# End of attention in an attention + two-MoE kernel: gates of the known rows in a product of their own, weight splits behind the last exponentials and ids, last pack's scores first

## The chip, the cores and the metric

The kernel runs on one core of a Trainium2 chip. The core has five engines that work side by side, each through its own queue in the order of the program: TensorE (PE in the rows; its weight loads are PEld), VectorE (DVE), ScalarE (ACT), GpSimd (POOL) and SyncE (SP, which here only reads registers and starts transfers). Sixteen DMA engines move data between the main memory and the on-chip memory. TensorE's clock is granted at one of two levels, 1.2 or 2.4 GHz; the rows give it as 0.5 or 1.0. The metric is the device time of one execution in microseconds (us), the median of several.

## The reference

Block-causal attention (2 sequences of 576 tokens, 8 heads of 64), whose output of 1152 rows x 512 goes through two mixture-of-experts (MoE) layers. Each layer gives a row to the expert with the largest logit (8 experts, weights 512x1024 and 1024x512), multiplies by a gate, and in the first layer by a second, sigmoid gate. The second layer has a capacity per expert.

```python
scores = np.where(block_i >= block_j, scale * q @ k.T, -1e9)      # blocks of 64
x = softmax(scores) @ v                                           # -> 1152 x 512
logits = x @ w_gate;  e_idx = argmax(logits, 1)
gate_w = softmax(logits)[arange, e_idx];  eom = sigmoid(x @ w_output_gate)
for e in range(E):                                                # first MoE
    h = relu(x[mask] @ w1[e]);  out[mask] = gate_w * eom[mask, e] * (h @ w2[e])
# second MoE: the same on its own weights, without eom, with a capacity per expert
```

## The kernel before

**Attention.** The nine query blocks of a head are put into three packs (numbers 0, 1, 2). For a pack PE computes scores into the tile `s` (`qk_steps`), DVE takes the negative row maximum `mx`, ACT the exponential `p`, PE transposes `p` into the tile `pst` (`transp`), ACT or DVE copies it out as `tp`, PE multiplies by the values (`pv`), ACT copies the result as `ot`, and PE turns it back with the logits of the first MoE beside it (the matrix `mv`). DVE divides by the row sums, into `x1` (the rows) and `lg` (the logits), and adds `lg` to `lg1`. The last two heads, 6 and 7, are interleaved: stages (6,0), (7,0), (6,1), (7,1), (6,2), (7,2). In a row such as `tp_7_2_0` the numbers are head, pack and group; `p1_2` is block 2 of an odd head, `p0_8` block 8 of an even one.

**Known rows.** When pack 0 of head 7 is done, 384 of the 1152 rows have all their logits. The routine `route_first` picks the expert that most of them have (its number is `e`) and finds, for up to 384 of these known rows, where they lie (`ids`), the gates (`gs`) and several tables (`kx`, `tx`, `bm`, `dl`, `oht`, `pi`) that the routing of the other rows needs later. It does so in small steps on DVE with products on PE between them: the counts (L289), the places (L320, L322: `a_selb` with a triangle of ones), then a selection by the one-hot matrix `a_ohp` (L369, L371). The last one has in one product the row numbers and the three bf16 parts of the gate, `rag`, five columns a row tile, each times three groups. Its result is read as `ids` (L374, L375), as the register `e2` (the expert again, L379) and as `gs` (L382). `begin_first` spreads these steps over the end of attention, one piece for each call of `extra_step`. It starts the load of the first weights (4 chunks of 512 KB into `raw`) as soon as `e` is known, gathers the known rows (`xg`, three gathers on POOL's queue) when `ids` is there, and then starts the load of the second weights, four more chunks.

**Splits.** The products of the MoE take float32 numbers as a high and a low part. `split_hi` (ACT, L169) casts a weight chunk to its high part `wh`; `split_lo` (DVE, L187) subtracts that to get `wl`. Chunk 0 of layer 1 is split inside `begin_first`, chunks 1 to 3 after the stages, each held behind an anchor instruction by `issue_after` (an order on one engine's queue, without a wait).

**Order and the start of the MoE.** Around here the order on each queue is made by a list scheduler from the order in which the program is written, these anchors and the dependencies; from `manual_schedule` on it is as written. The first MoE begins with the transposes of the first gathered tile, `px<-ident,xg` (L706). They wait for the gather, and their place in PSUM comes free with the last `lg` of attention (L1459 for head 7, pack 2). ACT then casts `xh`, and the 12 products of 512 columns `ph<-wh,xh` and so on (L719) of a half of layer 1 follow.

Of the kernel before, what the change touches and what calls it, by code (L numbers as in the profile page):

```python
# [8 lines left out]
F32 = mybir.dt.float32  # L9
# [5 lines left out]
ALU = mybir.AluOpType  # L15
AX = mybir.AxisListType
# [16 lines left out]
def kernel(  # L33
# [15 lines left out]
    nc = tc.nc  # L49
    V = nc.vector  # L50
# [4 lines left out]
    P = 128  # L55
# [127 lines left out]
    def split_lo(c, s=0, src=None):  # L183
        i = c + s * KD
        fill()
        fill()
        V.tensor_tensor(wls[i], raw[:, c, :] if src is None else src, whs[i].bitcast(F32), op=ALU.subtract)  # L187

    def split(c, s=0, src=None):

        w = split_hi(c, s, src)
        split_lo(c, s, src)
        return w
# [10 lines left out]
    def gather_rows(dst, table, ids):  # L204
        return nc.gpsimd.indirect_dma_start(out=dst, out_offset=None, in_=table, in_offset=bass.IndirectOffsetOnAxis(ap=ids.bitcast(U32), axis=0))
# [72 lines left out]
    def route_first(m, r, lg, og, eligible, tok, capacity, pst):  # L278
# [65 lines left out]
        yield 0  # L344
        ohp = sm([NA, P], "ohp", BF16)
        for t in range(NA):
            V.tensor_scalar(ohp[:, t, :], i128, pp[:, t : t + 1], BIG, op0=ALU.subtract, op1=ALU.is_equal)
            yield 0
        part = [sm([NA], f"part{i}", BF16) for i in range(3)]
        for _ in gates(sm, ex, og, oh, NA, part):  # L350
            yield 0
        ra = sm([NA, 5], "ra", BF16)
        for j, val in enumerate([thr[:, 0:NA], tok[:, 0:NA]] + part):
            V.tensor_copy(ra[:, :, j], val)
            yield 0
        rb = sm([2], "rb", BF16)
        V.tensor_copy(rb, pid.to_broadcast([P, 2]))
        if G > 1:
            yield 0
            og = ohg[:, :, 0:G].unsqueeze(2)  # L360
# [4 lines left out]
            V.tensor_scalar(rbg, og.to_broadcast([P, NA, 2, G]), pid[:, 0:1], None, op0=ALU.mult)  # L365
        yield 1
        ps = pst()
        for t in range(NA):
            nc.tensor.matmul(ps[:, 0 : 5 * G], ohp[:, t, :], ra[:, t, :] if G == 1 else rag[:, t].rearrange("p j g -> p (j g)"), start=(t == 0), stop=False)  # L369
# [5 lines left out]
        V.tensor_scalar_add(ids[:, G : 2 * G], ps[:, G : 2 * G], float(N))  # L375
        r["ig"], r["io"] = ids[:, 0:G], ids[:, G : 2 * G]
        if m == 1:

            V.scalar_tensor_tensor(out=er, in0=ps[:, 0:1], scalar=0.0, in1=ef, op0=ALU.mult, op1=ALU.add)  # L379
            r["e2"] = nc.sync.value_load(er[0:1, 0:1], min_val=0, max_val=E - 1)  # L380
        gs = sm([G], "gs")
        V.tensor_reduce(out=gs, in_=ps[:, 2 * G : 5 * G].rearrange("p (j g) -> p g j", j=3), op=ALU.add, axis=AX.X)  # L382
        r["gs"] = gs
        yield 1
        if m == 1:
            iof = sm([G], "iof")
            V.tensor_scalar_add(iof, ps[:, G : 2 * G], float(N))
            r["oht"], r["pi"] = spots(sm, iof, G)

        kx = sm([NT, E], "kx")  # L390
# [850 lines left out]
    with ExitStack() as actx:  # L1241
# [7 lines left out]
        def pst():  # L1249
            return ps_t.tile([P, 512], F32, tag="t", name="pst")  # L1250
# [156 lines left out]
        def transp(h, pk, g):  # L1407
            s = st[h]
            grp = [(b, c) for c, bs in groups[pk][g] for b in bs]
            ps = pst()  # L1410
            n = len(grp) * P
            for j, (b, c) in enumerate(grp):
                last[0] = nc.tensor.transpose(ps[:, j * P : (j + 1) * P], s["p"][b][:, c * P : (c + 1) * P], ident).ins  # L1413
# [51 lines left out]

        def begin_first():

            it = Phases(route_first(1, first1, lg1[:, 0:NA, 0:E], lg1[:, 0:NA, E : 2 * E], None, tok_t, None, pst))
# [11 lines left out]
            g = [gather_rows(xg, x1d[0 : NA * P, :], first1["ig"][:, i : i + 1]).ins for i, xg in enumerate(item0["xg"])][0]  # L1480
# [16 lines left out]
        def extra_step():  # L1497
            if behind:
                calls[0] += 1
                if calls[0] in (3, 4):  # L1500
                    return
            while extra:
                try:
                    if behind:
                        with tc.issue_after(last[0]):
                            next(extra[0])
                    else:
                        next(extra[0])
                    return
                except StopIteration:  # L1510
                    extra.pop(0)
# [41 lines left out]
        for i, (h, pk) in enumerate(stages):  # L1553
# [257 lines left out]
```

## Time and profile before

| | |
|---|---|
| median of 3 runs | 416.88 us (416.2 to 418.99) |
| the profiled execution, its own time | 416.57 us |
| its span in the trace | 414.8 us |
| PE / DVE / ACT / POOL busy, share of the span | 93% / 70% / 61% / 25% |
| mean granted TensorE clock | 0.976 of full speed |

The span is the time from the first to the last recorded instruction; what lies around it is 1.8 us. A timeline row has the start, the time from the first start to the last end of the instructions that it merges, the engine, the line, the operation, output and inputs, the count, and in brackets the idle time before it with what ended it. The busy time of PE includes its pipeline, so rows that follow each other overlap; the distance of two starts is what one costs. Attention ends near 140 us; layer 1 of the first MoE starts at 140.12 us.

### The profile page before, as it was taken

To read this page: it belongs to the slowest core of one execution; us is meant where nothing else is said; L and a number is where in the kernel's file an instruction comes from. 1 tells how busy PE (TensorE), PEld (TensorE's weight loads), DVE (VectorE), ACT (ScalarE), POOL (GpSimd) and SP (SyncE) were. 2 spreads that over 40 slices of the span, in tenths; PEclk is the share of its full clock that TensorE was granted. 3 is DMA by queue.
4 is the path that set the end of the run, shared out by engine and by line. 5 is a ranking of instruction groups with operands and counts; after the bars stand their busy time and mean duration, and the time that the engine had idled before them with its cause. 6 is when DMAs were issued, how large, how long until landed. Compare 5 with 4: busy or idle time off the path is not lost. (4 is left out here: it accounts for less than half of the span.)

```text
span 414.8 us, 7835 instructions
## 1 busy us (share of the span) xinstructions
PE 386.4 (93%) x2443; PEld 295.3 (71%) x2443; DVE 289.4 (70%) x755; ACT 254.1 (61%) x531; POOL 101.6 (25%) x211
## 2 busy tenths in 40 slices
PE   4899999999996899999999999978999999999992
PEld 3677887887775678888888866656777888856540
DVE  4577667766788697798988944679789999911010
ACT  2678778878775552877878611553679998821110
POOL 8452201212100204103212110121710287200100
PEclk9999999999997999999999999978899999999998
DMA  6649932510106802991661388360795999899890
GB/s 139 114 105 285 294 103 61 144 24 7 57 22 223 297 3 84 305 345 54 216 242 52 122 335 321 137 228 2 248 384 188 333 371 401 288 384 390 297 362 29
DMA packets 65111, 82.88 MB, mean 200 GB/s; under 512 B 34368, under 2 KB 38976, under 8 KB 65060
## 3 DMA queue, kind: packets, MB, share of 16 engines
q1 hardware_dynamic: 62180, 72.98, 52.4%
q0 software_dynamic: 2880, 9.31, 6.1%
q8 instruction: 21, 0.34, 0.3%
q14 instruction: 30, 0.25, 0.2%
HBM read 91.57 MB, written 11.80 MB: 249 GB/s over the span
## 5 line engine op out<-in xcount | busy, mean ns | idle before, releaser
L187 DVE TENSOR_TENSOR wl<-raw,wh 128x1024 fp32r<-128x1024 f32 x52 | 61.3, 1220 | 2.3 <-ACT wh L169 2.3
L169 ACT CAST wh<-raw 128x1024 fp32r<-128x1024 f32 x52 | 51.5, 1052 | 1.0 <-DMA raw<-in_moe_w_dram 0.8
L719 PE MATMUL ph<-wh,xh 128*128 128x512 f32 x120 | 50.7, 422 | 1.4 <-ACT xh L708 1.4
L719 PE MATMUL ph<-wh,xl 128*128 128x512 f32 x120 | 48.6, 405 | 0.0
L719 PE MATMUL ph<-wl,xh 128*128 128x512 f32 x120 | 48.2, 402 | 0.0
L1387 DVE TENSOR_REDUCE mx<-s 128x1 f32<-128x256 f32 (+8 forms) x72 | 34.4, 486 | 17.5 <-PE s L1386 4.6
L1390 ACT ACTIVATE p<-s,mx 128x256 f32<-128x256 f32 (+8 forms) x72 | 37.8, 527 | 10.1 <-DVE mx L1387 9.2
L1413 PE MATMUL pst<-ident,p 128*128 128x128 f32 x200 | 39.1, 291 | 0.4 <-DVE lg L1459 0.3
L187 DVE TENSOR_TENSOR wl_a<-raw,wh_a 128x1024 fp32r<-128x1024 f32 x28 | 33.2, 1220 | 0.3 <-ACT wh_a L169 0.2
L1439 PE MATMUL pst<-tp,vn 128*64 128x128 f32 (+2 forms) x384 | 32.8, 297 | 0.1
L169 ACT CAST wh_a<-raw 128x1024 fp32r<-128x1024 f32 x28 | 28.1, 1061 | 5.8 <-DMA raw<-in_moe_w_dram 5.7
L733 PE MATMUL py<-wh_a,hh 128*128 128x512 f32 x72 | 30.1, 418 | 0.0
L1413 PEld LDWEIGHTS pst<-ident,p 128*128 128x128 f32 x200 | 25.4, 150 | 6.1 <-issue 2.4
L1417 ACT COPY tp<-pst 128x384 f32<-128x384 f32 (+1 forms) x48 | 24.5, 533 | 8.2 <-PE pst L1413 7.9
L733 PE MATMUL py<-wh_a,hl 128*128 128x512 f32 x72 | 28.7, 399 | 0.6 <-DVE hl L814 0.6
L733 PE MATMUL py<-wl_a,hh 128*128 128x512 f32 x72 | 28.8, 401 | 0.0
L187 DVE TENSOR_TENSOR wl_b<-raw,wh_b 128x1024 fp32r<-128x1024 f32 x24 | 28.4, 1220 | 0.6 <-ACT wh_b L169 0.5
L1386 PE MATMUL s<-kh,qh 128*128 128x320 f32 (+3 forms) x64 | 26.0, 406 | 2.7 <-ACT p L1390 1.4
L719 PEld LDWEIGHTS ph<-wh,xh 128*128 128x128 f32 x120 | 23.2, 193 | 6.4 <-ACT xh L708 1.9
L738 POOL DMA_INDIRECT out_dram<-ys,ig x7 | 11.9, 1705 | 63.5 <-ACT ys L921 57.1
L719 PEld LDWEIGHTS ph<-wh,xl 128*128 128x128 f32 x120 | 23.1, 192 | 6.1 <-DVE xl L709 1.3
L1439 PEld LDWEIGHTS pst<-tp,vn 128*64 128x64 f32 x384 | 21.1, 142 | 8.7 <-issue 3.8
(353 smaller groups left out, 868.9 us busy)
## 6 DMA issues: line engine op xcount, KB each, us to landing
raw<-in_moe_w_dram SPq DMA_DIRECT2D x132, 512.0 KB
rx<-in_moe_w_dram SPq DMA_DIRECT2D x20, 512.0 KB
out_dram<-zrow SPq DMA_DIRECT2D x9, 256.0 KB
x2d<-zrow SPq DMA_DIRECT2D x9, 256.0 KB
kn<-in_k_dram SPq DMA_DIRECT2D x16, 128.0 KB
qn<-in_q_dram SPq DMA_DIRECT2D x16, 128.0 KB
vn<-in_v_dram SPq DMA_DIRECT2D x16, 128.0 KB
x1d<-x SPq DMA_DIRECT2D x3, 576.0 KB
```

The source lines that it names most:

```text
L169: nc.scalar.copy(whs[i], raw[:, c, :] if src is None else src)
L187: V.tensor_tensor(wls[i], raw[:, c, :] if src is None else src, whs[i].bitcast(F32), op=ALU.subtract)
L719: yield nc.tensor.matmul(out_, l[:, c * P : (c + 1) * P], r[:, cols], start=(c == 0 and j == 0), stop=(c == KD - 1 and j == 2))
L733: nc.tensor.matmul(y, l[:, cs], r[:, rs], start=(first and j == 0), stop=(last and j == 2))
L738: nc.gpsimd.indirect_dma_start(out=dest, out_offset=bass.IndirectOffsetOnAxis(ap=io.bitcast(U32), axis=0), in_=ys, in_offset=None, bounds_ ...
L1386: nc.tensor.matmul(ps[:, a:z], s[l][:, b, :], s[r][:, a - o : z - o], start=(j == 0), stop=(j == 2))
L1387: anchors["mx", h, pk] = V.tensor_reduce(out=s["mx"][:, t : t + 1], in_=ps[:, o : o + n], op=ALU.max, axis=AX.X, negate=True).ins
L1390: anchors["p", h, pk] = nc.scalar.activation(s["p"][b][:, 0:n], ps[:, o : o + n], AF.Exp, bias=s["mx"][:, t : t + 1], accum_out=s["sm"][:, ...
L1413: last[0] = nc.tensor.transpose(ps[:, j * P : (j + 1) * P], s["p"][b][:, c * P : (c + 1) * P], ident).ins
L1417: anchors["tp", h, pk] = nc.scalar.copy(fp, ps[:, 0:n]).ins
L1439: nc.tensor.matmul(po[r, 0 : n * BLK], nat["v"][h % NR["v"]][:, c, r], w[:, :, r], start=(c == 0), stop=(c == nc_ - 1))
```

## The change

In `route_first`, for the first MoE, the selection becomes two products. The first has only the two row-number columns (`rag[:, :, 0:2]`, six columns of output) beside the `rbg` product, and `ids`, `e2` and `iof` come from it. The gates, their three parts and the second product (`rag[:, :, 2:5]`, nine columns) come after that, then `gs`; `oht`, `pi` and the tables stand behind. `begin_first` issues the two later pieces behind `first1["found"]`, the step that writes `iof` (on DVE), and leaves the rest of the generator (`first1["more"]`: `oht`, `pi`, `kx`, `tx`, `ne`, `bm`, `dl`, `efs`) for the end. `extra_step` also skips its sixth call. In the stage before the last, all scores of the last pack are issued first; in the last stage one piece of `begin_first` is issued at once, behind the transposes of (6,2). All four `split_hi` now follow the stages: chunks 0 and 1 behind the last exponential `p` of (7,2), chunk 2 behind the last ACT copy `tp`, chunk 3 behind the last `ot`. The `split_lo` of chunk 0 is held behind `found`, those of 1 and 2 behind `weighed` (the second `rag`), and the rest of the generator behind the `split_lo` of chunk 2.

```diff
@@ route_first
-        for _ in gates(sm, ex, og, oh, NA, part):
-            yield 0
         ra = sm([NA, 5], "ra", BF16)
-        for j, val in enumerate([thr[:, 0:NA], tok[:, 0:NA]] + part):
+        for j, val in enumerate([thr[:, 0:NA], tok[:, 0:NA]] + (part if G == 1 else [])):
...
-            V.tensor_tensor(rag, ra.unsqueeze(3).to_broadcast([P, NA, 5, G]), og.to_broadcast([P, NA, 5, G]), op=ALU.mult)
+            V.tensor_tensor(rag[:, :, 0:2], ra[:, :, 0:2].unsqueeze(3).to_broadcast([P, NA, 2, G]), gg.to_broadcast([P, NA, 2, G]), op=ALU.mult)
...
+        if G > 1:
+            for _ in gates(sm, ex, og, oh, NA, part):
+                yield 0
+            for j, val in enumerate(part):
+                V.tensor_copy(ra[:, :, 2 + j], val)
+                yield 0
+            r["weighed"] = V.tensor_tensor(rag[:, :, 2:5], ...).ins
+            yield 1
+            ps = pst()
+            for t in range(NA):
+                nc.tensor.matmul(ps[:, 0 : 3 * G], ohp[:, t, :], rag[:, t, 2:5].rearrange("p j g -> p (j g)"), start=(t == 0), stop=(t == NA - 1))
+            yield 0
+            V.tensor_reduce(out=gs, in_=ps[:, 0 : 3 * G].rearrange("p (j g) -> p g j", j=3), op=ALU.add, axis=AX.X)
+            yield 1
@@ begin_first, extra_step
-            it.one()
-            for _ in it.small():
-                pass
-            yield
-            with tc.issue_after(g):
-                item0["w1"] = [split(0)]
+            for _ in range(2):
+                with tc.issue_after(first1["found"]):
+                    it.one()
+                    for _ in it.small():
+                        pass
+                yield
...
-                if calls[0] in (3, 4):
+                if calls[0] in (3, 4, 6):
@@ the loop over the stages, and what follows it
+            if i + 2 == len(stages):
+                for _ in qs_:
+                    pass
+            if i + 1 == len(stages):
+                last[0] = anchors["turn", H - 2, 2]
+                extra_step()
...
-        for c, (w, h, pk) in ((1, ("ot", H - 1, 1)), (2, ("tp", H - 1, 2)), (3, ("ot", H - 1, 2))):
-            with tc.issue_after(anchors[w, h, pk]):
-                item0["w1"].append(split(c) if c < KD - 1 else split_hi(c))
+        item0["w1"] = []
+        for c, w in enumerate(("p", "p", "tp", "ot")):
+            with tc.issue_after(anchors[w, H - 1, 2]):
+                item0["w1"].append(split_hi(c))
+            if c < KD - 1:
+                with tc.issue_after(first1["weighed" if c else "found"]):
+                    at = split_lo(c)
+        with tc.issue_after(at):
+            for _ in Phases(first1["more"]).small():
+                pass
```

The queues before and after, at three places. First ACT's queue at the end of attention, of the kernel before from the copy of (6,2)'s transposes on: `p1_2` is the last exponential of all, `wh0` to `wh2` are the high parts of the weight chunks, `tp_7_2_0` and `tp_7_2_1` the copies that the last product with the values needs.

```order
L1417 COPY tp_6_2_1_1977<-pst_1972 128x512
L169 CAST wh0_108<-raw_107 128x1024
L169 CAST wh1_109<-raw_107 128x1024
L1390 ACTIVATE p1_2_171,sm7_1598<-s_7_2_1890,mx7_1597 128x192
L1417 COPY tp_7_2_0_2035<-pst_2031 128x384
L1417 COPY tp_7_2_1_2045<-pst_2040 128x512
L169 CAST wh2_110<-raw_107 128x1024
```

The same place of ACT's queue with the change, from the copies `ot0` of (6,2) on:

```order
L1461 COPY ot0_189<-pst_2016 64x64
L1407 ACTIVATE p1_2_171,sm7_1598<-s_7_2_1890,mx7_1597 128x192
L169 CAST wh0_108<-raw_107 128x1024
L169 CAST wh1_109<-raw_107 128x1024
L1434 COPY tp_7_2_0_2014<-pst_2010 128x384
L1434 COPY tp_7_2_1_2024<-pst_2019 128x512
L169 CAST wh2_110<-raw_107 128x1024
```

The two casts `wh0` and `wh1` stood ahead of the last exponential and stand behind it now, ahead of the two copies. Next DVE's queue, of the kernel before, from the remainder `wl2` of the third chunk to the last sum of the logits `lg1`; `x1` and `lg` with `pst_2037` belong to (6,2), with `pst_2073` to (7,2).

```order
L187 TENSOR_TENSOR wl2_114<-raw_107,wh2_110 128x1024
L1457 TENSOR_TENSOR x1_145<-pst_2037,ri6_1402 128x3x64
L1459 TENSOR_TENSOR lg_6_2_2070<-pst_2037,ri6_1402 128x48
L1457 TENSOR_TENSOR x1_145<-pst_2073,ri7_1599 128x3x64
L1459 TENSOR_TENSOR lg_7_2_2130<-pst_2073,ri7_1599 128x48
L1461 TENSOR_TENSOR lg1_105<-lg1_105,lg_7_2_2130 128x48
```

With the change the remainders `wl0`, `wl1`, the step `a_gs` and `wl2` come first, then sixteen small steps of `route_first`, of which the last eight are shown, and then the last `x1` and `lg` of (7,2):

```order
L453 COPY a_efs_1_2142<-a_ef_1_1841 128x3
L272 TENSOR_TENSOR a_oht_1_2121<-a_gt_1_2119 128x27
L274 TENSOR_REDUCE a_pi_1_2123<-a_gt_1_2119 128x3
L411 SCALAR_TENSOR_TENSOR a_kx_1_2126<-a_kp_1_1911,a_kx_1_2126 128x24
L418 TENSOR_SCALAR a_tx_1_2129<-a_tx_1_2129 128x72
L436 TENSOR_TENSOR bms_100<-bms_100,a_ne_1_2132 128x64
L447 TENSOR_TENSOR a_dl_1_2136<-a_dl_1_2136,a_ne_1_2132 128x8
L275 SCALAR_TENSOR_TENSOR a_pi_1_2123<-a_pi_1_2123,a_iof_1_2007 128x3
L1474 TENSOR_TENSOR x1_145<-pst_2052,ri7_1599 128x3x64
L1476 TENSOR_TENSOR lg_7_2_2108<-pst_2052,ri7_1599 128x48
```

So all sixteen, which before stood several microseconds earlier and between other work, are now between `wl2` and the last `x1`. Last PE's queue of the kernel before, where (6,2) is transposed (`pst_1899`) and the places of the known rows are computed (L320):

```order
L1413 MATMUL pst_1868<-ident_68,p1_6_175 128x128
L1413 MATMUL pst_1899<-ident_68,p0_8_168 128x128
L1413 MATMUL pst_1899<-ident_68,p0_3_163 128x128
L1439 MATMUL pst_1905<-tp_7_1_0_1810,vn1_152 64x192 x2
L1413 MATMUL pst_1899<-ident_68,p0_2_162 128x128
L1439 MATMUL pst_1905<-tp_7_1_1_1859,vn1_152 64x128 x4
L1439 MATMUL pst_1905<-tp_7_1_2_1871,vn1_152 64x128 x2
L1386 MATMUL s_7_2_1890<-kh7_1595,qh1_155 128x256
L1386 MATMUL s_7_2_1890<-kl7_1596,qh1_155 128x256
L1386 MATMUL s_7_2_1890<-kh7_1595,ql1_157 128x256
L320 LDWEIGHTS ltri_74
L320 MATMUL pst_1913<-a_selb_1_1847,ltri_74 128x4
```

And with the change:

```order
L1430 MATMUL pst_1868<-ident_68,p1_6_175 128x128
L320 LDWEIGHTS ltri_74
L320 MATMUL pst_1904<-a_selb_1_1847,ltri_74 128x4
L322 LDWEIGHTS ones_bf_73
L322 MATMUL pst_1904<-a_selb_1_1847,ones_bf_73 128x3
```

The places of the known rows moved ahead of the transposes of (6,2), the product with the values of (7,1) and the scores of 256 columns.

## Rows read from the trace of the kernel before

**Rows 1.** Page, part 2: TensorE's granted clock in 40 equal slices.
```profile
PEclk9999999999997999999999999978899999999998
```
**Rows 2.** Busy us (count) of each engine by stretch, PEclk, DMA share, GB/s.
```profile
126.71:128.87 2.16, 0.58 (x4) 0.41 (x3) 2.16 (x18) 1.92 (x5) 0.00 (x0) 1.00 0.85 332
128.87:135.70 6.83, 5.56 (x41) 4.37 (x43) 5.13 (x20) 2.85 (x6) 1.49 (x2) 0.50 0.40 146
135.70:140.12 4.42, 2.92 (x32) 2.27 (x28) 2.40 (x7) 2.96 (x9) 2.36 (x3) 1.00 0.94 329
...
275.64:282.47 6.83, 6.83 (x28) 5.07 (x28) 5.14 (x25) 2.84 (x4) 0.12 (x1) 0.50 0.23 89
289.30:292.71 3.41, 3.41 (x10) 2.64 (x9) 3.41 (x4) 3.19 (x4) 3.10 (x2) 0.50 0.31 82
```
**Rows 3.** Timeline of PE at the end of attention and the start of the MoE.
```profile
122.42 0.60 PE L1413 MATMUL pst<-ident,p 128*128 128x128 f32 x4
122.95 0.55 PE L1439 MATMUL pst<-tp,vn 128*64 128x192 f32 x4
...
123.69 0.88 PE L1439 MATMUL pst<-tp,vn 128*64 128x128 f32 x12
125.06 0.39 PE L1386 MATMUL s<-kh,qh 128*128 128x256 f32 x1 [0.49 <-ACT p L1390]
...
125.51 0.18 PE L320 MATMUL pst<-a_selb,ltri 128*128 128x4 bf16 x1
...
127.16 0.27 PE L1386 MATMUL s<-kh,ql 128*128 128x192 f32 x1
130.14 0.19 PE L369 MATMUL pst<-a_rag,a_ohp 128*128 128x15 bf16 x1 [2.71 <-DVE a_ohp L347]
...
138.78 0.63 PE L706 MATMUL px<-ident,xg 128*128 128x128 f32 x4 [0.68 <-DVE lg L1459]
140.12 0.50 PE L719 MATMUL ph<-wh,xh 128*128 128x512 f32 x1 [0.72 <-ACT xh L708]
```
**Rows 4.** Timeline of DVE in the same stretch.
```profile
122.78 0.75 DVE L1387 TENSOR_REDUCE mx<-s 128x1 f32<-128x576 f32 x1
...
124.96 0.18 DVE L317 TENSOR_REDUCE a_selb<-a_oe 128x3 bf16<-128x24 f32 x1
...
127.70 0.28 DVE L399 SCALAR_TENSOR_TENSOR a_tx<-a_eo,a_kq,thr 128x72 f32<-128x72 f32 x1
...
128.67 1.22 DVE L187 TENSOR_TENSOR wl<-raw,wh 128x1024 fp32r<-128x1024 f32 x1
...
133.45 0.16 DVE L374 CAST a_ids<-pst 128x3 int32<-128x3 f32 x1 [0.99 <-PE pst L371]
...
138.20 0.36 DVE L1457 TENSOR_TENSOR x<-pst,ri 128x192 f32<-128x192 f32 x1 [0.35 <-PE pst L1454]
```
**Rows 5.** Timeline of ACT in the same stretch.
```profile
129.50 0.41 ACT L1390 ACTIVATE p<-s,mx 128x192 f32<-128x192 f32 x1
...
134.46 0.59 ACT L1417 COPY tp<-pst 128x512 f32<-128x512 f32 x1 [2.45 <-PE pst L1413]
134.94 1.05 ACT L169 CAST wh<-raw 128x1024 fp32r<-128x1024 f32 x1
```
**Rows 6.** Timeline of PE elsewhere: a product with values, layer 1 at either clock.
```profile
103.93 1.22 PE L1439 MATMUL pst<-tp,vn 128*64 128x192 f32 x20
...
141.42 0.39 PE L719 MATMUL ph<-wl,xh 128*128 128x512 f32 x1
141.65 0.40 PE L719 MATMUL ph<-wh,xl 128*128 128x512 f32 x1
...
278.05 0.63 PE L719 MATMUL ph<-wh,xh 128*128 128x512 f32 x1
278.48 0.63 PE L719 MATMUL ph<-wl,xh 128*128 128x512 f32 x1
```
**Rows 7.** The tile `a_ids`, us from the issue of a gather to its landing.
```profile
DMA to landing us min/median/max: 4.6/6.7/7.1
```

More of the change, by code (lines that the diff above doesn't have):

```diff
@@ L186, in split_lo @@
         fill()
-        V.tensor_tensor(wls[i], raw[:, c, :] if src is None else src, whs[i].bitcast(F32), op=ALU.subtract)
+        return V.tensor_tensor(wls[i], raw[:, c, :] if src is None else src, whs[i].bitcast(F32), op=ALU.subtract).ins
     def split(c, s=0, src=None):
@@ L359, in route_first @@
             yield 0
-            og = ohg[:, :, 0:G].unsqueeze(2)
+            gg = ohg[:, :, 0:G].unsqueeze(2)
             rag = sm([NA, 5, G], "rag", BF16)
-            V.tensor_tensor(rag, ra.unsqueeze(3).to_broadcast([P, NA, 5, G]), og.to_broadcast([P, NA, 5, G]), op=ALU.mult)
+            V.tensor_tensor(rag[:, :, 0:2], ra[:, :, 0:2].unsqueeze(3).to_broadcast([P, NA, 2, G]), gg.to_broadcast([P, NA, 2, G]), op=ALU.mult)
             yield 0
             rbg = sm([NA, 2, G], "rbg", BF16)
-            V.tensor_scalar(rbg, og.to_broadcast([P, NA, 2, G]), pid[:, 0:1], None, op0=ALU.mult)
+            V.tensor_scalar(rbg, gg.to_broadcast([P, NA, 2, G]), pid[:, 0:1], None, op0=ALU.mult)
         yield 1
         ps = pst()
+        n = 5 if G == 1 else 2 * G
         for t in range(NA):
-            nc.tensor.matmul(ps[:, 0 : 5 * G], ohp[:, t, :], ra[:, t, :] if G == 1 else rag[:, t].rearrange("p j g -> p (j g)"), start=(t == 0), stop=False)
+            nc.tensor.matmul(ps[:, 0:n], ohp[:, t, :], ra[:, t, :] if G == 1 else rag[:, t, 0:2].rearrange("p j g -> p (j g)"), start=(t == 0), stop=False)
         for t in range(NA):
@@ L374, in route_first @@
         V.tensor_copy(ids[:, 0:G], ps[:, 0:G])
-        V.tensor_scalar_add(ids[:, G : 2 * G], ps[:, G : 2 * G], float(N))
+        r["found"] = V.tensor_scalar_add(ids[:, G : 2 * G], ps[:, G : 2 * G], float(N)).ins
         r["ig"], r["io"] = ids[:, 0:G], ids[:, G : 2 * G]
@@ L380, in route_first @@
             r["e2"] = nc.sync.value_load(er[0:1, 0:1], min_val=0, max_val=E - 1)
+            iof = sm([G], "iof")
+            r["found"] = V.tensor_scalar_add(iof, ps[:, G : 2 * G], float(N)).ins
         gs = sm([G], "gs")
-        V.tensor_reduce(out=gs, in_=ps[:, 2 * G : 5 * G].rearrange("p (j g) -> p g j", j=3), op=ALU.add, axis=AX.X)
         r["gs"] = gs
+        if G == 1:
+            V.tensor_reduce(out=gs, in_=ps[:, 2 * G : 5 * G].rearrange("p (j g) -> p g j", j=3), op=ALU.add, axis=AX.X)
         yield 1
+        if G > 1:
+            for _ in gates(sm, ex, og, oh, NA, part):
+                yield 0
+            for j, val in enumerate(part):
+                V.tensor_copy(ra[:, :, 2 + j], val)
+                yield 0
+            r["weighed"] = V.tensor_tensor(rag[:, :, 2:5], ra[:, :, 2:5].unsqueeze(3).to_broadcast([P, NA, 3, G]), gg.to_broadcast([P, NA, 3, G]), op=ALU.mult).ins
+            yield 1
+            ps = pst()
+            for t in range(NA):
+                nc.tensor.matmul(ps[:, 0 : 3 * G], ohp[:, t, :], rag[:, t, 2:5].rearrange("p j g -> p (j g)"), start=(t == 0), stop=(t == NA - 1))
+            yield 0
+            V.tensor_reduce(out=gs, in_=ps[:, 0 : 3 * G].rearrange("p (j g) -> p g j", j=3), op=ALU.add, axis=AX.X)
+            yield 1
         if m == 1:
-            iof = sm([G], "iof")
-            V.tensor_scalar_add(iof, ps[:, G : 2 * G], float(N))
             r["oht"], r["pi"] = spots(sm, iof, G)
@@ L1412, in transp @@
             for j, (b, c) in enumerate(grp):
-                last[0] = nc.tensor.transpose(ps[:, j * P : (j + 1) * P], s["p"][b][:, c * P : (c + 1) * P], ident).ins
+                last[0] = anchors["turn", h, pk] = nc.tensor.transpose(ps[:, j * P : (j + 1) * P], s["p"][b][:, c * P : (c + 1) * P], ident).ins
             tp = ap4.tile([P, 4, P], F32, tag="tp", name=f"tp_{h}_{pk}_{g}")
@@ L1466, in begin_first @@
         def begin_first():
-            it = Phases(route_first(1, first1, lg1[:, 0:NA, 0:E], lg1[:, 0:NA, E : 2 * E], None, tok_t, None, pst))
+            first1["more"] = route_first(1, first1, lg1[:, 0:NA, 0:E], lg1[:, 0:NA, E : 2 * E], None, tok_t, None, pst)
+            it = Phases(first1["more"])
             for i in range(4):
@@ L1479, in begin_first @@
             item0["xg"] = [XG.next() for _ in range(KN[1])]
-            g = [gather_rows(xg, x1d[0 : NA * P, :], first1["ig"][:, i : i + 1]).ins for i, xg in enumerate(item0["xg"])][0]
+            for i, xg in enumerate(item0["xg"]):
+                gather_rows(xg, x1d[0 : NA * P, :], first1["ig"][:, i : i + 1])
             load_w(w11, w12, first1["e2"], KD, 8)
             yield
-            it.one()
-            for _ in it.small():
-                pass
-            yield
-            with tc.issue_after(g):
-                item0["w1"] = [split(0)]
+            for _ in range(2):
[4 more added lines that the diff above has]
+                yield
         extra = []
```

3 lines of the change are left out of this document (2 added, 1 removed).

## The prediction

> **What bounds the kernel now.** I began with the clock's row of the page [rows 1]. It dips in the slices from 124 to 134 us, from 270 to 300 us and in the last; the first dip lies where the change works. By stretch [rows 2], the clock is full until 128.87, half from there to 135.70, and full again after. PE is busy for only 0.58 of the 2.16 us before the fall. The timeline of PE says why [rows 3]: its last score product starts at 127.16 and ends near 127.43, and the next product (L369, the selection of the known rows) starts at 130.14, after 2.71 us in which PE waited for `a_ohp` from DVE. DVE was late because a weight remainder `wl` of 1.22 us stood ahead of it [rows 4]. So the clock fell 1.44 us after PE had gone idle, and the 5.56 us of busy PE that follow up to 135.70 ran at half.
>
> The second thing to see is where the MoE begins. The transposes `px` start at 138.78, after 0.68 us in which PE waited for the last `lg` on DVE, and `ph`, the first product of layer 1, starts 1.34 us later, at 140.12 [rows 3]. From there on I count every microsecond of PE in full, since its rows follow each other without a pause (starts 0.23 us apart [rows 6]). So two numbers decide: when `ph` starts, and at which clock.
>
> **The change, part by part.** *The early part.* The row numbers now need neither gates nor parts. On DVE the maximum at 122.78 takes 0.75 us [rows 4] and ends at 123.5; in the new queue only one small step, one copy and two reciprocals stand between it and `a_selb`. That step cannot start before 123.5 and before the change started at 124.96 [rows 4]; I take 124.3, nearer the late end because the copy is no small step. PE now has L320 right behind two of the four transposes that start at 122.42 [rows 3], so it is idle from about 122.9 to 124.5: **a new pause of 1.6 us** (0.8 to 2.3 by the same two bounds). Before, other products lay there.
>
> From 124.5 on, PE has until the end of the id products: ten transposes at 0.13 us (four start at 122.42, the next work at 122.95), the products with values of (7,1) at 0.5 and 0.9 us (rows of 122.95 and 123.69), scores of 0.45 us (125.06 to 125.51), and some ten tiny products, 0.4 us by estimate [rows 3]. Sum 3.6 us: 128.1. `ids` then comes at about 128.4 in place of 133.45 [rows 4]: 5 us sooner. This buys little. The gathers take 4.6 to 7.1 us from issue to landing [rows 7], and the first was in time for 138.78 before; now it lands by 136 and nobody waits for it. The second weights come 5 us sooner too, and no row of PE shows a wait for them in layer 1.
>
> *The last exponential.* Behind the ids PE waits for `ot` and turns (7,1) back, 0.8 us (0.4 to 1.2, taken in the middle), multiplies (6,2) by the values, 1.2 us [rows 6], and does the last scores, 0.45 us: 130.5. With the maximum on DVE (0.5 us) the last `p` starts at 131.1. Before it started at 129.50 [rows 5]: though its block is issued first, it is 1.6 us later, because the pause and the id products now lie ahead of it.
>
> *From there to `ph`.* ACT now has `wh0` and `wh1` between the last exponential and the two copies `tp` of (7,2), and `wh2` behind these. DVE has `wl2` and sixteen small steps ahead of the last `x1` and `lg`. In order: `p` 0.5 us, two casts at 1.05, two copies (0.59 and about 0.45), the cast `wh2` 1.05 [rows 5], its remainder `wl2` 1.22, sixteen small steps, and 0.58 from the last `x1` (138.20) to `px` (138.78) [rows 3, 4]. For the sixteen I use the 18 DVE instructions of the 2.16 us from 126.71, 0.12 us each, 1.9 us [rows 2]; the longest of them took 0.28 alone [rows 4]. Sum: 0.5 + 2.1 + 1.05 + 1.05 + 1.2 + 1.9 + 0.6 = 8.4 us, so `px` at 139.5 against 138.78 and `ph` at 140.8 against 140.12: **+0.7 us**. The other branch (`ot` behind `wh2`, the turn back, `x1`) would be ready for `x1` near 137, so it is DVE that is late next. Casts and small steps were covered before, by PE's pause and by its slow stretch; that cover is gone.
>
> *The clock.* Between 132 and 140.8 PE now has pauses of about 2 us (for the copies behind `wh0`, `wh1`), 0.8 us (for `ot`), 2.5 us (for the last `lg`) and 0.8 us (for `xh`), and less than 3 us of work. Before, from 135.70 to 140.12, it was busy for 2.92 of 4.42 us and the clock stayed full; a fall came with 0.58 busy of 2.16 [rows 2]. The new stretch is nearer the second. So layer 1 most likely starts at half clock. Its products start 0.43 us apart there, 0.23 at full [rows 6], so each microsecond at half loses 0.47. Dense work ran 3.41 and 6.83 us at half before the clock came back [rows 2]: 1.6 or 3.2 us lost. I take the middle, **+2.4 us**; the bounds are nothing and 3.2.
>
> The sum is made against the profiled execution's own time, 416.57 us (span 414.8 and 1.8 around it), 0.3 below the median 416.88: 416.57 + 0.7 + 2.4 = 419.7 us.
>
> **Rule and row.** The trace shows a fall 1.44 us after PE went idle, inside a pause of 2.71 us [rows 2, 3]. The Trainium skill (TensorE: Matmul & The Clock Gate, section "HAM oscillation — how this bites in real kernels") gives as its abstract rule that only pauses longer than any of these cost the clock. By it there would be no fall before, which the rows contradict, and none with the change, which gives the time of the first rival.
>
> **The rivals.** *The clock holds.* If pauses with short work between them do not let it fall, only the shift stays: 416.57 + 0.7 = 417.3 us. For it speaks that 135.70 to 140.12, with pauses of 0.7 us, kept the full clock; against it that PE will be busy for much less there. *Slower: the new pause at 122.9 also lets the clock fall.* Its place is L320 behind `a_selb`; it decides if the clock falls in that pause as it did in the one at 128.87. Then the 3.6 us of work up to `ids` runs at 1.9 times its length, wholly or in part: 0 to 3.1 us, middle 1.6, and all behind it is late: 421.3 us. For it speaks the estimate of 1.6 us; against it that PE worked densely right before and after. *Faster: the clock holds and DVE's small steps are cheap.* If they and `wl2` slip in before the last turn back is done, `px` comes when that branch allows, near 137.6, 1.1 us sooner than before: 415.4 us. For it speaks that the stall of 2.71 us is gone; against it the fixed order, in which `wl2` cannot start before the third cast. That the change does nothing is no case here, since `ids` must come sooner; only its use is in doubt.
>
> **How the numbers follow.** Chances: layer 1 at half clock alone 0.42 (419.7), with the early fall too 0.28 (421.3), the clock holds 0.17 (417.3), faster 0.13 (415.4). The likeliest gives the prediction, 419.7. The range goes from the faster case, 415.4, to the early fall with its upper half, 422.3. About 1%, 4.2 us, is what a measurement of this kernel can tell from no change. Slower by more, over 421.05, takes somewhat over half of the early fall and a little of the likeliest with a long low stretch: 0.24. Faster by more, under 412.7, needs the faster case and that the low stretch of 289.30 to 292.71 [rows 2] goes as well, which is worth 1.6 us, and more: 0.04. The rest, 0.72, is within 1%.
>
> **What would show it.** Right: PE waits for `a_selb` before L320 for about 1.6 us; `ids` near 128.4; the last exponential near 131; ACT's copies of (7,2) directly behind two casts; DVE without a pause from `wl2` to the last `x1`; `px` waiting for `lg` near 139.5; and layer 1 with starts 0.43 us apart for 3 to 7 us. Wrong: `px` well before 138, a full clock from 135 to 143, or a wait of layer 1 for weights or gathers, none of which I expect.

## The result, and the profile after

| | before | after |
|---|---|---|
| median, us | 418.01 (415.82 to 419.91) | 422.01 (418.80 to 425.10) |
| ratio of times, 95% interval | | 1.0092 [1.0067, 1.0118] |
| profiled execution: time, span, mean clock | 416.57, 414.8, 0.976 | 421.62, 419.8, 0.967 |

The change costs 0.9%, 4 us. Both medians were taken side by side; the line numbers of the changed kernel are up to 17 higher behind the edit (L706 is L723, L719 is L736, L1439 is L1456, L369 is L371, L374 is L376, L1457 is L1474).

The granted clock of the page, which answers to [rows 1]:

```profile
PEclk9999999999998599999999999988899999999998
```

The first dip is longer and deeper than before; its two slices hold two falls of the clock. The stretches (length, busy us of PE, PEld, DVE, ACT and POOL with counts, PEclk, DMA share, GB/s), which answer to [rows 2]:

```profile
122.90:126.12 3.22, 1.45 (x15) 1.01 (x15) 2.75 (x19) 1.31 (x3) 0.00 (x0) 1.00 0.40 90
126.12:129.53 3.41, 3.41 (x19) 2.24 (x18) 1.25 (x5) 0.59 (x1) 0.00 (x0) 0.50 0.97 380
129.53:136.36 6.83, 5.09 (x53) 4.08 (x54) 6.11 (x35) 5.25 (x16) 3.37 (x4) 1.00 0.66 229
136.36:139.77 3.41, 2.66 (x25) 2.29 (x23) 3.41 (x16) 2.44 (x5) 0.00 (x0) 0.50 1.04 400
139.77:146.60 6.83, 5.42 (x16) 3.92 (x16) 4.08 (x17) 0.91 (x3) 0.00 (x0) 0.50 0.37 129
```

In this stretch the clock falls twice: at 126.12 for 3.41 us and at 136.36 for 10.24 us. Before, it fell once here, for 6.83 us, and was full when layer 1 began. PE's timeline, for [rows 3]:

```profile
124.67 0.18 PE L320 MATMUL pst<-a_selb,ltri 128*128 128x4 bf16 x1 [1.77 <-DVE a_selb L317]
...
135.86 0.55 PE L1456 MATMUL pst<-tp,vn 128*64 128x192 f32 x4 [1.71 <-ACT tp L1434]
...
138.81 0.90 PE L1470 MATMUL pst<-mv,ot 128*128 128x160 f32 x2 [0.75 <-ACT ot L1461]
...
140.75 1.09 PE L723 MATMUL px<-ident,xg 128*128 128x128 f32 x4 [0.69 <-PE pst L1471]
142.56 0.80 PE L736 MATMUL ph<-wh,xh 128*128 128x512 f32 x1 [0.72 <-ACT xh L725]
143.15 0.63 PE L736 MATMUL ph<-wl,xh 128*128 128x512 f32 x1
143.58 0.63 PE L736 MATMUL ph<-wh,xl 128*128 128x512 f32 x1
...
147.30 0.60 PE L723 MATMUL px<-ident,xg 128*128 128x128 f32 x4
```

The stall of 2.71 us is gone, and three others have come: 1.77, 1.71 and 0.75 us (the 0.69 us ahead of `px` was 0.68 before). The second fall, at 136.36, comes 0.5 us after the pause of 1.71 us has ended; the pauses of 0.75 and 0.69 us lie behind it. `px` starts 1.97 us later than before and `ph` 2.44 us later. The products of layer 1 start 0.43 us apart until 146.56. The second `px`, which marks the end of the first half of layer 1, is at 147.30; before it was here:

```profile
143.26 0.60 PE L706 MATMUL px<-ident,xg 128*128 128x128 f32 x4
```

This 4.04 us stays: the `px` that starts at 266.32 before starts at 270.41, and the one at 381.24 at 385.37. The two spans differ by 5.05 us; the last us or so arises behind that, where the code is the same (PE's last products start at 410.65 against 405.84). DVE and ACT, for [rows 4] and [rows 5]:

```profile
124.43 0.18 DVE L317 TENSOR_REDUCE a_selb<-a_oe 128x3 bf16<-128x24 f32 x1
...
130.28 0.15 DVE L376 CAST a_ids<-pst 128x3 int32<-128x3 f32 x1
...
135.16 2.36 DVE L187 TENSOR_TENSOR wl<-raw,wh 128x1024 fp32r<-128x1024 f32 x2
...
137.51 1.22 DVE L187 TENSOR_TENSOR wl<-raw,wh 128x1024 fp32r<-128x1024 f32 x1
...
140.11 0.15 DVE L275 SCALAR_TENSOR_TENSOR a_pi<-a_pi,a_iof 128x3 f32<-128x3 f32 x1
140.18 0.35 DVE L1474 TENSOR_TENSOR x<-pst,ri 128x192 f32<-128x192 f32 x1
```

```profile
133.03 0.42 ACT L1407 ACTIVATE p<-s,mx 128x192 f32<-128x192 f32 x1 [0.33 <-DVE mx L1404]
...
133.45 1.98 ACT L169 CAST wh<-raw 128x1024 fp32r<-128x1024 f32 x2
135.33 0.97 ACT L1434 COPY tp<-pst 128x384 f32<-128x384 f32 x2
136.18 1.06 ACT L169 CAST wh<-raw 128x1024 fp32r<-128x1024 f32 x1
```

Here the reader sees the forecast chain: after the last exponential ACT does two casts, and only then the copies that PE waits 1.71 us for; DVE goes without a pause from `wl` to the last `x`.

### The profile page after: what moved, and what is told of

Same layout as the page of the kernel before. It is cut to its first block, busy times and chain, and to the rows that moved or that the text cites. A ratio compares the mean times of both kernels' runs of the same rounds, so it can differ in the third digit from the quotient of the medians.

```text
span 419.8 us, 7843 instructions
## 1 busy us (share of the span) xinstructions
PE 389.7 (93%) x2446; PEld 298.2 (71%) x2446; DVE 289.9 (69%) x756; ACT 254.9 (61%) x531; POOL 102.0 (24%) x211
## 5 line engine op out<-in xcount | busy, mean ns | idle before, releaser
L736 PE MATMUL ph<-wh,xh 128*128 128x512 f32 x120 | 51.5, 429 | 1.4 <-ACT xh L725 1.4
L736 PE MATMUL ph<-wh,xl 128*128 128x512 f32 x120 | 49.0, 408 | 0.0
L736 PE MATMUL ph<-wl,xh 128*128 128x512 f32 x120 | 48.8, 407 | 0.0
L1456 PE MATMUL pst<-tp,vn 128*64 128x128 f32 (+2 forms) x384 | 33.8, 299 | 1.8 <-ACT tp L1434 1.7
L1456 PEld LDWEIGHTS pst<-tp,vn 128*64 128x64 f32 x384 | 21.4, 142 | 10.2 <-issue 4.1
L736 PEld LDWEIGHTS ph<-wh,xh 128*128 128x128 f32 x120 | 23.7, 197 | 6.7 <-ACT xh L725 2.0
L736 PEld LDWEIGHTS ph<-wh,xl 128*128 128x128 f32 x120 | 23.4, 195 | 6.0 <-DVE xl L726 1.1
```

Source lines behind the costliest of these rows:

```text
L736: yield nc.tensor.matmul(out_, l[:, c * P : (c + 1) * P], r[:, cols], start=(c == 0 and j == 0), stop=(c == KD - 1 and j == 2))
L1456: nc.tensor.matmul(po[r, 0 : n * BLK], nat["v"][h % NR["v"]][:, c, r], w[:, :, r], start=(c == 0), stop=(c == nc_ - 1))
```

## The experiments

The theory was that of the prediction: the chain behind the last exponential holds `px`, and the pauses that it makes in PE drop the clock for layer 1. Its rivals: the clock does not matter; the product of its own does the harm; the order of the scores does it. A ratio is always to the kernel before, run on the same chip in the same hours. The start of one and the same row near 120 us lies from 119.71 to 120.01 in the profiles (119.41 in `paced`, 117.92 in `ids_alone`), so differences under 0.3 us between starts mean nothing, and the rows of those two are early by about as much.

### The pauses filled: fill_early, fill_late, fill_both

Products of 512 columns that nobody reads were put into PE's pauses, their order fixed by `issue_after` (these excerpts and those below are shortened, with comments of mine).

```diff
+        def dummies(n, after):            # dm: one free PSUM tile of the scores' pool
+            for _ in range(n):
+                with tc.issue_after(after):
+                    after = nc.tensor.matmul(dm[0][:, 0:512], kh7[:, 0:P], kh7[:, 0:512], start=True, stop=True).ins
+            return after
# early: ahead of L320, behind the transposes of pst_1868
+        last[0] = dummies(7, anchors["turn", H - 1, 1])
# late: ahead of the last pack's pv, its mv, and px
+        dummies(7, anchors["turn", H - 1, 2, 1])
+        dummies(2, anchors["pv", H - 1, 2])
+        dummies(6, anchors["back", H - 1, 2])
```

> The changed kernel with seven products of 512 columns (0.23 us each at full clock, 1.6 us in all) that nobody reads, put on PE between the transposes of (7,1) and L320, where it pauses 1.77 us for a_selb. Orders of the other engines are those of the changed kernel. Theory (the pause lets the clock fall, and the fall makes all that follows late): no half clock between 123 and 131 us, the ids about 1.7 us sooner than 130.28, layer 1 still at half clock at its start; 1 to 1.7 us under the changed kernel, 420.3 to 421.0 where that has 422.0. Rival (the fall near 126 is harmless, because ACT's casts and DVE set the pace behind it): 421.7 to 422.3.

> The changed kernel with such unread products in its late pauses on PE: seven while it waits for the copies of (7,2) behind the two casts, two while it waits for ot, six while it waits for the last lg. Theory (layer 1 starts at half clock because of these pauses): full clock from 136 us on, layer 1 with starts 0.23 us apart from its first product, its start no later than in the changed kernel; 2 to 3 us under the changed kernel, 419.0 to 420.0. Rival (the loss is in the late start alone and the half clock is made good by later waits): 421.7 to 422.3.

> Both fills together: the changed kernel at full clock from attention through layer 1. Theory: only the later start is left. With the early fall gone px starts near 139.5 and ph near 140.8, +0.7 us against the kernel before, which itself has its own fall; 418.3 to 419.0, 3 to 3.7 us under the changed kernel. Rival (the order costs more than the clock): 420.5 or above.

Measured: early alone 1.0074 [1.0039, 1.0110], late alone 1.0020 [0.9985, 1.0056], both 1.0005 [0.9972, 1.0039]. As ratios to the 418.01 us of before, the theory gave 1.0055 to 1.0072, 1.0024 to 1.0048 and 1.0007 to 1.0024, so late and both came out a little lower than forecast, and early between theory and rival, which its interval does not tell apart. PE with the early pause filled:

```profile
134.60 0.55 PE L1456 MATMUL pst<-tp,vn 128*64 128x192 f32 x4 [1.71 <-ACT tp L1434]
136.89 0.57 PE L1470 MATMUL pst<-mv,ot 128*128 128x160 f32 x2 [0.75 <-ACT ot L1461]
139.38 1.09 PE L723 MATMUL px<-ident,xg 128*128 128x128 f32 x4 [1.58 <-issue]
...
145.39 0.60 PE L723 MATMUL px<-ident,xg 128*128 128x128 f32 x4
```

(Behind "issue" the profile shows no releaser; the last `lg` on DVE ends at 139.28.) With the late ones filled:

```profile
124.87 0.18 PE L320 MATMUL pst<-a_selb,ltri 128*128 128x4 bf16 x1 [1.77 <-DVE a_selb L317]
...
144.92 0.60 PE L723 MATMUL px<-ident,xg 128*128 128x128 f32 x4
```

and with both:

```profile
132.49 1.86 PE L1579 MATMUL dummy<-kh 128*128 128x512 f32 x7
...
138.94 0.66 PE L723 MATMUL px<-ident,xg 128*128 128x128 f32 x4
...
143.46 0.60 PE L723 MATMUL px<-ident,xg 128*128 128x128 f32 x4
```

With the early pause filled only the late fall is left (at 137.27), with the late ones filled only the early fall (at 126.53), with both the clock is full until 275.95. The second `px` splits the 4.04 us: 147.30 - 145.39 = 1.91 for the early fall, 145.39 - 143.46 = 1.93 for the late one, and 143.46 - 143.26 = 0.20 for everything else. Taken in the other order, by way of the late fill, it is 144.92 - 143.46 = 1.46 for the early fall and 147.30 - 144.92 = 2.38 for the late one. Almost the whole loss is the clock's. In the medians the late fall weighs more (0.7%, 2.9 us) and the early one less (0.2%, 0.8 us) than in these single executions; their intervals allow both. (The profiled execution of `fill_late` is the longest of its ten, 421.56 us against a median of 418.79: a `px` that is 2.40 us ahead of the changed kernel's at 268.01 is followed by one only 1.00 us ahead at 299.30.) That the change without a fall only equals the kernel before says that its earlier ids and its other order bring no gain of their own that shows.

### One part of the change: ids_alone, paced

`ids_alone` is the kernel before with the product of its own and nothing else. `paced` is the changed kernel without the three lines that issue the last pack's scores first:

```diff
-            if i + 2 == len(stages):
-                for _ in qs_:
-                    pass
```

> The kernel before with one part of the change alone: the gates of the known rows in a product of their own (three more products of 9 columns on PE, rag made in two pieces); weight splits, scores and all other work stand where they stood before. Theory (the product of its own costs nothing by itself; the loss comes from the moved splits and the order of the scores, and from the clock): 0.998 to 1.002 of before, px within 0.3 us of 138.78, the stall ahead of L371 still there at 2.5 to 2.8 us. Rival (the second product or its reduction holds px up): 1.004 or more.

> The changed kernel without the four lines that issue all scores of the last pack first; the rest of the change stays (two products, casts behind the last exponential, remainders behind the ids). By the order of its queues L320 stands behind the transposes of (6,2) and the product with values of (7,1) again, and on DVE the last x1 and lg stand ahead of wl1, wl2 and the sixteen small steps. Theory (the change loses by what stands ahead of the last exponential and the last lg): no pause before L320, last exponential near 128.5, px near 136, layer 1 from about 137.3; 414 to 416.5. Rival (the second product and the casts behind the last exponential are what costs): 420 to 422, like the changed kernel.

`ids_alone`: 1.0013 [0.9989, 1.0036]. Its rows lie earlier by 1.8 us from the start (`a_selb` 123.16 against 124.96), so `px` at 137.32 answers to 139.1, 0.3 us late, the edge of what I gave. The stall is still there:

```profile
128.44 0.19 PE L371 MATMUL pst<-a_rag,a_ohp 128*128 128x6 bf16 x1 [2.78 <-DVE a_ohp L347]
```

By the time, the product of its own costs nothing that shows. `paced` gave 1.0069 [1.0035, 1.0103], a miss for my theory, which wanted a gain. PE and DVE there:

```profile
135.65 0.23 PE L400 MATMUL pst<-a_rag,a_ohp 128*128 128x9 bf16 x3 [1.46 <-DVE a_rag L396]
138.51 1.11 PE L723 MATMUL px<-ident,xg 128*128 128x128 f32 x4 [2.63 <-DVE a_gs L402]
```

```profile
135.51 2.35 DVE L187 TENSOR_TENSOR wl<-raw,wh 128x1024 fp32r<-128x1024 f32 x2
...
138.30 0.16 DVE L402 TENSOR_REDUCE a_gs<-pst 128x3 f32<-128x9 f32 x1
```

The early pause is gone and the ids come at 129.63, but `px` waits for the reduction of the gates, `a_gs`, and this stands behind two remainders and some small steps on DVE. So a wait that the other order had hidden comes up; the clock falls at 136.56, behind the pause of 1.46 us and 0.7 us into the one of 2.63, and layer 1 starts at half clock all the same. So the loss does not need the scores issued first. The scores first alone, in the kernel before, no run has; the next runs keep them first and move the rest.

### The casts and the small steps in another place: casts_only, smalls_only, casts_moved

```diff
-        for c, w in enumerate(("p", "p", "tp", "ot")):
-            with tc.issue_after(anchors[w, H - 1, 2]):
+        for c, w in enumerate((("p", H - 1, 2, packs[2][0][0]), ("tp", H - 1, 2), ("ot", H - 1, 2), ("ot", H - 1, 2))):
+            with tc.issue_after(anchors[w]):            # casts_only, casts_moved
                 item0["w1"].append(split_hi(c))
...
-        with tc.issue_after(at):
+        with tc.issue_after(anchors["lg", H - 1, 2]):   # smalls_only, casts_moved
             for _ in Phases(first1["more"]).small():
```

> The changed kernel with the four casts of wh alone in another place (wh0 behind the first exponential of the last pack, wh1 behind tp, wh2 and wh3 behind ot); the small operations keep their program order behind the splits, nothing is filled in. Theory (the two casts of 2.0 us between the last exponential and the copies of tp make PE's pauses of 1.71 and 0.75 us, and with them the second fall of the clock): these pauses are under 0.6 us, the clock stays at 1.00 between the early fall and 275 us, and the time is 0.999 to 1.004 of before. Rival (it was the small operations ahead of x and lg): still 1.006 to 1.011.

> The changed kernel with the sixteen small operations of DVE behind the last x and lg, the casts where the change put them. Theory (the casts bring the loss, the small operations 1.5 us of DVE that partly lie beside PE's half-clock work): the pause of 1.7 us ahead of pv and the second fall of the clock stay, px moves by less than 1 us, the time is 1.005 to 1.010 of before. Rival (the small operations hold px): 0.999 to 1.004.

> The changed kernel with the casts and the small operations in another place, nothing filled in: the cast of wh0 behind the first exponential of the last pack, wh1 behind the two copies of tp, wh2 and wh3 behind the three copies of ot, and the sixteen small operations of DVE behind the last x and lg. Theory of the prediction (px is set by the chain behind the last exponential, in which two casts of 2.0 us, wl2 and the small operations stand ahead of tp and x): the copies of tp come 2 us earlier after the last exponential, px comes 1 to 2.5 us earlier than 140.75, and with the clock as in the change the time is 1.002 to 1.006 of before. Rival (the chain does not matter while the clock is low; PE's own work at half clock sets px): 1.007 to 1.011.

Measured: `casts_only` 1.0050 [1.0011, 1.0089], `smalls_only` 1.0079 [1.0047, 1.0111], `casts_moved` (both moves) 1.0005 [0.9970, 1.0040]. PE with the small steps alone moved:

```profile
124.79 0.18 PE L320 MATMUL pst<-a_selb,ltri 128*128 128x4 bf16 x1 [1.77 <-DVE a_selb L317]
...
134.66 0.55 PE L1456 MATMUL pst<-tp,vn 128*64 128x192 f32 x4 [1.71 <-ACT tp L1434]
136.94 0.64 PE L1470 MATMUL pst<-mv,ot 128*128 128x160 f32 x2 [0.75 <-ACT ot L1461]
...
138.60 1.09 PE L723 MATMUL px<-ident,xg 128*128 128x128 f32 x4 [0.67 <-PE pst L1471]
```

and with both moved:

```profile
135.24 1.38 PE L1456 MATMUL pst<-tp,vn 128*64 128x192 f32 x20 [0.35 <-ACT tp L1434]
137.38 0.54 PE L1470 MATMUL pst<-mv,ot 128*128 128x160 f32 x2 [0.42 <-ACT ot L1461]
138.78 0.63 PE L723 MATMUL px<-ident,xg 128*128 128x128 f32 x4 [0.68 <-PE pst L1471]
...
143.85 0.60 PE L723 MATMUL px<-ident,xg 128*128 128x128 f32 x4
```

The pauses of 1.71 and 0.75 us shrink to 0.35 and 0.42 with both moved and do not shrink with the small steps alone, so the casts make them. With both moved the profile has no late fall, `px` is back at the 138.78 of before, and the loss is gone though nothing is filled in; the early pause and its fall (at 125.09) remain. The time is below the 1.002 to 1.006 that I gave, since I had left the late fall in. (The mean clock of its executions runs from 0.968 to 0.983, so in others it may have fallen more.) This shows the cause of the late part: the place of the casts and small steps, by way of PE's pauses. How it divides between the two is not settled. Moving the small steps alone brings `px` to 138.60, against 139.38 in `fill_early`, which like it has the late fall alone (here at 137.25). `casts_only` landed a little outside the range that I gave it (0.999 to 1.004); its one profile had a fall at 139.40, behind `px`, but it is of a long execution (422.72 us, the median is 419.71) and I draw nothing from it. The two moves alone give back 0.4% and 0.1%, together 0.9%, with intervals of about 0.35% each.

### Both remedies, and the kernel before with its own pause filled: casts_moved_fill, fill_before

`casts_moved_fill` adds 7, 4, 2 and 2 unread products at the four places to `casts_moved`. `fill_before` puts 11 of them ahead of L369 into the kernel before:

```diff
+                if (h, pk, b) == (H - 1, 2, packs[2][-1][0]):
+                    dummies(11, scored)
```

> The same as the kernel with the casts moved, and unread products of 512 columns in PE's pauses: 7 ahead of L320, 4 ahead of the last pack's pv, 2 ahead of its mv and 2 ahead of px. Theory (chain and clock add up): the clock stays at 1.00 from 16 to about 275 us, px starts 1 to 2.3 us before the 138.94 of the kernel with all pauses filled, and the time is 0.994 to 0.998 of before, faster than both kernels. Rival (DVE's total work, three wl of 1.2 us and the x and lg, sets px wherever it stands): px within 0.4 us of 138.94 and the time 0.999 to 1.002 of before.

> The kernel before with one thing added: 11 products of 512 columns that nobody reads stand on PE in its own pause of 2.71 us ahead of L369 (127.43 to 130.14 us in the profile of before). Theory (the granted clock follows what PE did in the pause ahead, and the half-clock stretch costs time in both kernels): the clock stays at 1.00 past 128.87, the 5.56 us of PE work that stood at half clock get shorter by 1 to 2 us, the ids come earlier than 133.45 and px earlier than 138.78 by 0.7 to 2.0 us: 0.995 to 0.998 of the time before. Rival (PE's work there lies beside the casts, the splits and the gathers anyway): the clock stays up and px does not move, 0.999 to 1.002. If the unread products hold L369 up by their own length, 1.002 or more.

`casts_moved_fill`: 0.9975 [0.9938, 1.0013]; full clock until 276.61, and

```profile
137.43 0.63 PE L723 MATMUL px<-ident,xg 128*128 128x128 f32 x4 [0.17 <-PE dummy L1579]
```

so `px` comes 1.5 us earlier than with the pauses filled alone (138.94), in the middle of the range of the theory, and the median is clearly below that of the changed kernel. Against the kernel before it is the fastest that I had, but its interval takes in no change.

`fill_before`: 1.0008 [0.9973, 1.0042], a miss: I wanted a gain of 0.2 to 0.5%. PE and the stretches:

```profile
138.11 0.63 PE L706 MATMUL px<-ident,xg 128*128 128x128 f32 x4 [1.74 <-DMA xg<-x1d,a_ids]
...
144.11 0.60 PE L706 MATMUL px<-ident,xg 128*128 128x128 f32 x4
```

```profile
130.14:135.70 5.56, 4.83 (x63) 3.84 (x62) 5.06 (x21) 3.63 (x13) 2.22 (x3) 1.00 0.54 150
135.70:140.06 4.36, 1.90 (x11) 1.24 (x10) 1.83 (x8) 1.56 (x2) 1.17 (x2) 1.00 1.04 395
140.06:143.47 3.41, 3.41 (x9) 2.61 (x9) 2.27 (x7) 0.26 (x1) 0.00 (x0) 0.50 1.01 365
```

The old fall is gone and the ids come at 132.41 in place of 133.45. But PE, now faster, is done before the gather and waits 1.74 us for it, and behind this longer pause (PE busy for 1.90 of the 4.36 us before the fall) the clock falls after all, at 140.06, for 3.41 us of layer 1. The gain is given back on the spot: `px` is 0.67 us earlier than before, the second `px` 0.85 us later. This suggests that in the kernel before the ids are close to being the bound: `px` comes 5.3 us behind them there (133.45, 138.78) and 5.7 us here, where it waits for the gather.

### Without the scores first, and the gates ahead of the remainders: casts_moved_paced, casts_moved_paced_fill

`casts_moved` without the scores first (as `paced`), and `wl1` and `wl2` held behind `a_gs`; the second with 6 unread products ahead of `px`:

```diff
-                with tc.issue_after(first1["weighed" if c else "found"]):
+                with tc.issue_after(first1["summed" if c else "found"]):   # summed: the reduction into gs
...
+        dummies(6, anchors["back", H - 1, 2])                              # the second alone
```

> The kernel with casts and small operations moved, without the rule that puts the last pack's scores first (they stand between the others as before), and with wl1 and wl2 behind the reduction of the gates (L402), which px had waited for in the run without the scores first. Theory (the product of its own gives ids 3 us earlier, and nothing stands ahead of tp, x and the gates' reduction any more): no early pause and no early fall, px at 136.3 to 137.5, 1.3 to 2.5 us before the kernel before; a pause of 1 to 2 us ahead of px may still drop the clock. 0.994 to 0.999 of before. Rival (the gather of xg or the gates hold px where it was): px at 138.3 or later and 0.999 to 1.004.

> The same with 6 unread products of 512 columns on PE behind the last mv, in the pause ahead of px. Theory: no fall of the clock from 17 to about 275 us, px within 0.4 us of the kernel without the fill, 0.992 to 0.997 of before, the fastest of all. Rival (the pause was too short to drop the clock, or PE is not what layer 1 waits for): the same as without the fill within 0.002.

Measured: 1.0051 [1.0017, 1.0085] and 1.0044 [1.0007, 1.0080], both misses. In the first the gates are late again, PE waits for them, and the clock falls at 136.01 for 10.24 us, all through the first half of layer 1:

```profile
137.09 0.24 PE L400 MATMUL pst<-a_rag,a_ohp 128*128 128x9 bf16 x3 [1.86 <-DVE a_rag L396]
137.87 1.11 PE L723 MATMUL px<-ident,xg 128*128 128x128 f32 x4 [0.53 <-DVE a_gs L402]
```

In the second the clock holds and `px` comes early, but layer 1 then waits for DVE, which is at the two remainders and reaches `xl` only behind them:

```profile
137.83 0.66 PE L723 MATMUL px<-ident,xg 128*128 128x128 f32 x4 [0.55 <-DVE a_gs L402]
...
140.91 0.50 PE L736 MATMUL ph<-wh,xl 128*128 128x512 f32 x1 [0.97 <-DVE xl L726]
...
143.32 0.60 PE L723 MATMUL px<-ident,xg 128*128 128x128 f32 x4
```

So the second `px`, at 143.32, is where it was before, and by this profile the time should be that of before. The median is 0.4% above. The profiled execution (417.58 us, mean clock 0.983) is one of the shortest of its kernel, and most of the others had a lower mean clock; which stretch they lost it in is not recorded, so the difference stays open.

## Why the prediction held, point by point

The forecast 419.7 us was 0.75% over its profiled execution; measured were 0.92% [0.67, 1.18], inside the range and on the forecast side, by the mechanism that was forecast. The profiled execution, 421.62 us, is the rival in which the clock also falls early (421.3).

The total came nearer than its terms, and that is in part luck. By the profiles the likeliest sum leaves out an early fall of 1.9 us (1.5 in the other order), has the late fall at 2.4 where it cost 1.9 (2.4), and has 0.7 for the shift where 0.2 is left; what is missing and what is too much partly cancel. The upper end of the range, 422.3, does not come out of its terms either: with the upper half of the early fall (1.6 to 3.1, so 2.35) the likeliest time is 422.05. Nothing hangs on it.

- **The new pause, right.** 1.6 us forecast, 1.77 measured; `a_selb` at 124.43 against 124.3.
- **The ids, right where the clock holds.** 128.4 forecast; 128.74 with both pauses filled, 130.28 in the changed kernel, whose early fall stretches the work ahead of them. That they buy little holds for the changed kernel. It was too general: `fill_before` waits for the gather.
- **The last exponential, right in kind.** 131.1 forecast; 131.62 with both filled, 133.03 with the early fall.
- **The chain behind it, somewhat too long.** 8.4 us forecast; 140.75 - 133.03 = 7.7 in the changed kernel, 138.94 - 131.62 = 7.3 with a full clock. The sixteen small steps take 1.5 us (138.65 to 140.18), not 1.9. The last pause, forecast at 2.5 us, is 0.69 in the changed kernel, where the turn back ahead of it runs at half clock, and 1.58 in `fill_early`. A late start and a short chain cancelled: `px` was forecast at 139.5 and comes at 138.94 (full clock) or 139.38 (late fall alone). That the casts and small steps in the chain are the cause, `casts_moved` shows.
- **The clock in layer 1, right that it falls, too large in its part there.** +2.4 us forecast behind `ph`. Measured from `ph` to the second `px`: 147.30 - 142.56 = 4.74 in the changed kernel, 144.92 - 141.79 = 3.13 with the late pauses filled, so 1.6 us. I had not counted that the same fall, at 136.36, also stretches the last turn back, `px` and the wait for `xh` ahead of `ph`.
- **The early fall, the right price at too small a chance.** Its price was 1.6 us (0 to 3.1), measured 1.91 or 1.46 by the profiles; its chance 0.28. It fell in the profiled execution, and likewise in those of `fill_late`, `casts_moved` and `casts_only`, but not in that of `smalls_only` with the same pause. Eleven of the fourteen executions of the changed kernel have a mean clock of 0.965 to 0.969, like the profiled one (0.967), so it probably fell in most. But two of the other three, at 0.974 and 0.975, the level of `fill_early` (0.975), took 421.76 and 422.52 us, about the median (422.01), so what it costs in the median stays open. The argument against it, dense work right before and after, was no protection.
- **Rule and row.** The Trainium skill's abstract rule (TensorE: Matmul & The Clock Gate, section "HAM oscillation — how this bites in real kernels") lets only pauses longer than any seen here cost the clock. The trace disagrees again: the clock fell behind a pause of 1.77 us, and again 0.5 us after one of 1.71 us.
- **The faster rival** (415.4: small steps slip in beside the turn back) did not come by itself. `px` reached 137.43, where that rival had it (137.6), only with casts and small steps moved by hand and the pauses filled.

## What to carry to other kernels

An operation moved off the path of one engine may open a pause in another: price the pause by the clock of the work behind it, not by its own length, here 3.8 of the 4.0 us in the profiles. To find out, put unread products into the pause; if the time comes back, look for what made the pause, since removing that (here the casts ahead of the copies and the small steps behind them) did as much without them. And when a stall is removed, ask what it was covering: here the gather in the one kernel, the gates' reduction in the other.

## What the runs showed of the hardware

- **The same pause drops the clock in one execution and not in another.** The pause of 1.77 us ahead of L320 (1.78 in two of them) was followed by a fall in the profiles of the changed kernel (at 126.12; PE busy for 1.45 of the 3.22 us before it), `fill_late` (126.53), `casts_moved` (125.09) and `casts_only` (125.75), and by none in that of `smalls_only`, whose program differs from the changed kernel's only later, on DVE. Over the executions of the changed kernel that were compared the mean clock runs from 0.965 to 0.975.
- **Unread products hold the clock.** In `fill_both` 7 in the pause of 1.77 us and 7, 2 and 6 in those of 1.7, 0.75 and 0.7 us or more kept it full until 275.95. They held up what stood behind them by 0.4 us at most (with both filled the last `lg` starts at 138.29 and `px` 0.65 later; in the changed kernel 0.30 us lie between).
- **A half-clock stretch cannot be priced by itself.** With the 6.83 us at half clock before the change filled away, `px` came 0.67 us earlier, and a new fall behind PE's wait for the gather took that back. What the time would be with that wait filled too, no run shows.
